# A capped attention with a gated layer behind it: a slightly different hand-written order, a smaller first table, a shorter warm-up, and the last three products in column halves

## The chip, the cores and the metric

The kernel runs on one core of a Trainium2 chip. Its time is device microseconds of one execution; a kernel's time is the median of several runs. Besides, one execution was recorded by the hardware profiler, with a start and a length for every instruction. The engines that matter here are TensorE (products, and weight loads that run beside them), VectorE, ScalarE, GpSimd (little used) and SyncE, whose queue issues most transfers.

## The reference

Four batches of twelve heads, 448 positions, head size 64. The attention's scores are capped by a tanh, and its output goes, heads side by side, through a gated layer whose gate mixes positions:

```python
scores = (1 / sqrt(64)) * q @ k.T
scores = cap * tanh(scores / cap)                # cap = 30
attn = exp(scores - max(scores)); attn /= sum(attn) + 1e-9
x = heads_side_by_side(attn @ v)                 # 4 x 448 x 768

h = gelu_tanh(x @ w_in)                          # 768 -> 1024
u, v = h[..., :512], h[..., 512:]
v_n = (v - mean(v)) / sqrt(var(v) + 1e-6) * g_ln
v_s = w_sg @ v_n + b_sg[:, None]                 # over the 448 positions
out = x + (u * v_s) @ w_out                      # 512 -> 768
```

## The kernel before

The kernel takes two heads (a pair, "batch.pair") at a time, six pairs a batch. Keys stand on the partitions of the scores, in three chunks of 128 and a tail of 64 for two pairs together. For each chunk TensorE makes the scores of both heads (`score`), ScalarE makes a tanh (L615) and an exp (L617) of 128x896 each, and TensorE multiplies by the values (`value`, L576; tails L586). The softmax denominators are made on TensorE too, with a table of ones (`sum`, L468), after VectorE has added some of the exps (`add`, L628). No maximum is subtracted, since the cap bounds the scores.

Most products are made from two rounded parts of each operand, three products for one (`TERMS`); VectorE or ScalarE makes the parts (`qk hi`, L523 or L526, and `qk lo`, L530). Others are plain fp32 products, which need four passes: the values, the sums, score tails (L552), and the scores of a few pairs in the list `PLAIN` (L560).

The gated layer of a batch runs among the attention of the batches that follow: `hv` (L759), `hu` (L814), `vsg` (L831) and `out` (L851) on TensorE, with gelu, layer norm and gate on the other engines between them (`cube` L742, `gelu` L747, `g hi` L306 or L308, `g lo` L334). The weights come as float64 words and are decoded on the chip (lines 380 to 420) while the attention runs.

TensorE's products use four shapes of tile: 128x128 for the gated layer, 64x128 for scores, 128x32 for values and sums, 64x64 for tails. The kernel's program gives each operation the letter of its shape as a mode.

Nothing decides the order at run time. All operations are built first, each with what it reads and writes, and then issued in an order that is written out as the tuple `ORDER`: each entry is twice the operation's number, plus 1 for the second of its two possible engines (ScalarE in place of VectorE). Every engine and every queue keeps its operations in that order and waits at the first whose data isn't there. Costs such as `PASS`, `PASS4` and `ISSUE` are those of the search that made the order; the run doesn't use them.

At the start TensorE runs a few products on zeros (`warm`, L365, `WARM` = 3 products of two records each). The first score's keys come as a small table `first` of their own, with the cap in a 129th column. Three small operations on VectorE (`scales`, L341 to L343) make from the cap the factors that tanh and exp need, and one on GpSimd the factor for the split of queries and keys. The other constants (ones, norm factors) come as a table `consts`. The first pair's queries are issued on ScalarE's queue, all other loads on SyncE's.

At the end the last pair of row blocks goes: `out 5.0` to `out 5.3` of the last batch, each three products of 448 columns into one accumulator; then `residual 5a` and `5b` on VectorE add half the columns each, and a store on SyncE's queue and one on ScalarE's write them out.

## Time and profile before

| | |
|---|---|
| median of 3 runs | 371.4 us (371.33 to 371.82) |
| profiled execution, its own time | 371.88 us |
| its span, first to last instruction | 370.1 us |
| TensorE products busy | 364.8 us |
| VectorE busy | 305.5 us |
| ScalarE busy | 224.1 us |

The span is what the trace covers; about 1.8 us of the execution's time lie around it. A product's end in the trace is modelled and reaches beyond its place in the pipeline, so that the busy time of TensorE also holds short waits. Starts are measured.

### The profile page before, as it was taken

The page shows a single profiled execution, that of the slowest core. Times are in us where ns is not written, and L with a number is a line of the kernel's source. Part 1 is how long each engine was busy: PE and PEld are TensorE (multiplying, and loading weights), DVE is VectorE, ACT ScalarE, POOL GpSimd, SP SyncE. Part 2 cuts the span into 40 slices and gives each one's busy share as a digit, 9 for nine tenths or more (in the row PEclk, how much of TensorE's full clock was granted, in tenths as well). Part 3 has the DMA queues.
Part 4 walks back from the last instruction along what each step waited for, and adds up shares of the span by engine and source line. Part 5 has one row for each costly group of instructions (what it writes and reads, how often), then busy time and mean ns, then how long its engine had stood idle before and what let it go on. Part 6 is the DMA issues. An engine that isn't in the chain of part 4 may idle for free.

```text
span 370.1 us, 6066 instructions
## 1 busy us (share of the span) xinstructions
PE 364.8 (99%) x2324; PEld 248.5 (67%) x2324; DVE 305.5 (83%) x548; ACT 224.1 (61%) x297; POOL 37.6 (10%) x39
## 2 busy tenths in 40 slices
PE   9999999999999999999999999999999999999995
PEld 4333343445778485546558986486889999889995
DVE  3999999999999999999997876986459789167663
ACT  5999999999566878998853528851024330041310
POOL 0303211120301310211000100000001000001000
PEclk9999999999999999999999999999999999999999
DMA  7978254545354214652513401001210000002204
GB/s 268 349 259 279 77 192 167 151 158 160 87 151 128 64 45 139 215 180 69 155 49 115 135 0 49 0 27 60 81 51 25 25 27 26 27 0 75 101 0 149
DMA packets 23996, 39.88 MB, mean 108 GB/s; under 512 B 5568, under 2 KB 18592, under 8 KB 23968
## 3 DMA queue, kind: packets, MB, share of 16 engines
q1 hardware_dynamic: 23680, 39.16, 33.3%
q8 instruction: 18, 0.29, 0.3%
q10 hardware_dynamic: 288, 0.34, 0.3%
q14 instruction: 10, 0.08, 0.1%
HBM read 33.47 MB, written 6.02 MB: 107 GB/s over the span
## 4 chain that ended last, share of the span: by engine, by line
PE 81%; DVE 12%; ACT 2%; issue 2%; DMA 2%; DVEq 0%; ACTq 0%
PE ps L814 12%; PE ps L576 11%; PE ps L851 11%; PE sc L544 9%; PE ps L759 8%; PE ps L831 5%; PE sc L851 5%; PE sc L759 4%; PE sc L814 4%; DVE p L628 3%; PE den L468 3%; PE sc L831 2%; PE sc L552 2%; PE ps L586 2%; DMA n<-spread 2%
## 5 line engine op out<-in xcount | busy, mean ns | idle before, releaser
L617 ACT ACTIVATE p<-p,few 128x896 f32<-128x896 f32 x84 | 85.2, 1047 | 0.5
L628 DVE TENSOR_TENSOR p<-p,p 128x896 f32<-128x896 f32 (+1 forms) x58 | 64.1, 1107 | 4.4 <-PE ps L576 3.0
L615 ACT ACTIVATE p<-sc 128x896 f32<-128x896 f32 x63 | 56.3, 919 | 9.6 <-PE sc L544 6.3
L576 PE MATMUL ps<-p,v 128*32 128x448 f32 x576 | 62.0, 544 | 0.0
L544 PEld LDWEIGHTS sc<-hl 64*128 64x128 f32 x378 | 32.4, 184 | 28.2 <-ACT p L615 15.9
L544 PE MATMUL sc<-hl 64*128 64x448 f32 x378 | 48.8, 385 | 0.0
L814 PE MATMUL ps<-rg,winu 128*128 128x448 f32 x206 | 46.5, 363 | 0.0
L851 PE MATMUL ps<-rg,wout 128*128 128x448 f32 x180 | 45.0, 366 | 0.0
L759 PE MATMUL ps<-winv,rg 128*128 128x512 f32 x170 | 42.6, 391 | 0.0
L814 PEld LDWEIGHTS ps<-rg,winu 128*128 128x128 f32 x206 | 38.5, 188 | 3.3 <-issue 0.3
L413 POOL TENSOR_TENSOR stage<-stage 128x512 int32<-128x512 int32 (+1 forms) x20 | 28.2, 1410 | 113.5 <-DVE stage L403 81.7
L576 PEld LDWEIGHTS ps<-p,v 128*32 128x32 f32 x576 | 15.6, 109 | 35.7 <-issue 20.8
L851 PEld LDWEIGHTS ps<-rg,wout 128*128 128x128 f32 x180 | 33.3, 188 | 5.0 <-issue 1.3
L759 PEld LDWEIGHTS ps<-winv,rg 128*128 128x128 f32 x170 | 31.7, 188 | 7.1 <-DVE rg L334 0.7
L740 ACT ACTIVATE t<-ps 128x448 f32<-128x448 f32 (+1 forms) x22 | 12.5, 567 | 28.6 <-PE ps L814 17.6
L745 ACT ACTIVATE t<-t 128x448 f32<-128x448 f32 (+1 forms) x30 | 18.0, 603 | 19.4 <-DVE t L742 19.3
L774 POOL TENSOR_TENSOR sm<-sm,few 128x1 f32<-128x1 f32 x14 | 8.7, 622 | 182.8 <-DVE sm L772 104.1
L831 PE MATMUL ps<-wsg,rg 128*128 128x448 f32 x116 | 26.7, 366 | 0.0
L740 ACT ACTIVATE t<-sc 128x512 f32<-128x512 f32 (+1 forms) x8 | 4.5, 571 | 34.8 <-PE sc L759 31.9
L530 DVE SCALAR_TENSOR_TENSOR hl<-raw,few,hl 128x848 fp32r<-128x848 f32 x21 | 24.4, 1162 | 0.1
L831 PEld LDWEIGHTS ps<-wsg,rg 128*128 128x128 f32 x116 | 21.5, 188 | 3.2 <-issue 1.0
L615 ACT ACTIVATE p<-sc,few 128x896 f32<-128x896 f32 x21 | 20.9, 1009 | 3.8 <-PE sc L560 1.9
(118 smaller groups left out, 511.8 us busy)
## 6 DMA issues: line engine op xcount, KB each, us to landing
raw<-in_qk_dram SPq DMA_DIRECT2D x22, 456.0 KB
stage<-in_w_in_dram SPq DMA_DIRECT2D x12, 512.0 KB
n<-spread SPq DMA_DIRECT2D x24, 224.0 KB
v<-in_vp_dram SPq DMA_DIRECT2D x24, 192.0 KB
out_dram<-x SPq DMA_DIRECT2D x17, 224.0 KB
stage<-in_w_out_dram SPq DMA_DIRECT2D x8, 384.0 KB
out_dram<-x SPq DMA_DIRECT2D x13, 112.0 KB
u<-in_w_sgT_dram SPq DMA_DIRECT2D x4, 224.0 KB
```

The source lines that it names most:

```text
L413: nc.gpsimd.tensor_tensor(out=a.bitcast(I32), in0=a.bitcast(I32), in1=hi, op=ALU.add)
L530: op(name("qk lo", s), "dve", c_tt(n) + 0.06, lambda: nc.vector.scalar_tensor_tensor(out=part(1), in0=used(), scalar=root, in1=f32(part(0) ...
L544: nc.tensor.matmul(out=sc.t[:, h, :S], lhsT=flat(s, w)[rows, 128 * c - 128:128 * c], rhs=flat(s, m)[rows, Q0 - TL:SQ - TL], start=(k == 0) ...
L576: nc.tensor.matmul(out=pav[s].t[32 * j:32 * j + 32, :S], lhsT=v[s].t[:, 128 * (c - 1) + 32 * j:128 * (c - 1) + 32 * j + 32], rhs=p.t[:, j ...
L615: op(name("tanh", s, c), "act", c_act(2 * S, True, raw_scores), lambda p=p, sc=sc, r=raw_scores: nc.scalar.activation(out=p.t, in_=sc.t[:, ...
L617: op(name("exp", s, c), "act", c_act(2 * S, False, True), lambda p=p: nc.scalar.activation(out=p.t, in_=p.t, func=ACTF.Exp, scale=cap_sb), ...
L628: op(name("add", s, t), "dve", c_tt(2 * S), lambda: nc.vector.tensor_tensor(out=a.t[rows], in0=a.t[rows], in1=p.t[rows], op=ALU.add), rd=[ ...
L745: op(tag + " tanh", "act", c_act(n), lambda: nc.scalar.activation(out=view(), in_=view(), func=ACTF.Tanh, scale=GELU_C * GELU_A), wr=[sq])
L759: nc.tensor.matmul(out=ps.t[:, :HF], lhsT=(xl if a else xh)[c].t[:, t * 128:t * 128 + 128], rhs=win[w][1][:, c, :], start=(c == 0 and k == ...
L814: nc.tensor.matmul(out=ps.t[:, :S], lhsT=win[w][0][:, c, f * 128:(f + 1) * 128], rhs=(xl if a else xh)[c].t[:, :S], start=(c == 0 and k == 0),
L831: nc.tensor.matmul(out=ps.t[:, :S], lhsT=(vl if a else vh)[c].t[:, f * 128:(f + 1) * 128], rhs=wsg[w][:, c, :], start=(c == 0 and k == 0), ...
L851: nc.tensor.matmul(out=ps.t[:, :S], lhsT=wout[w][:, f, c * 128:(c + 1) * 128], rhs=(gl if a else gh)[f].t[:, :S], start=(f == 0 and k == 0 ...
```

## The change

1. `ORDER` is another one. No operation is added but one (below), and what each computes is the same. On TensorE 208 of 525 steps keep their rank and the others move by 1.8 places in the mean, 21 at most. Twenty-five operations change between VectorE and ScalarE, among them the splits `3.1 qk hi`, `3.3 qk hi` and `3.4 qk hi`, which go to ScalarE. On SyncE's queue the constants are issued second, ahead of the keys and queries that had stood before them.
2. The cap moves from the first table, which now has 128 columns (512 bytes a row), into a new last column of the constants. So `scales` reads, and waits for, the constants.
3. The warm-up's products have 272 columns in place of 296.
4. The step `out 5.3` of the last batch becomes `out 5.3a` and `out 5.3b`, three products each on one half of the columns, and `residual 5a` waits for the first half alone.
5. The search's costs `PASS` and `PASS4` are lower.

Some neighbourhoods of the new order that the prediction speaks of, by the names of the steps:

- At the head TensorE's order is score 1, 2, 3, tail score, value 1, then `sum 0` and two scores of pair 0.1; before, value 2 stood ahead of `sum 0`.
- `0 hu 0.0` stood behind `0 hv 2.5`; now three `hu` steps run ahead of that one. On VectorE `1 den sum` and `1 recip` stood ahead of `0 v 0 gelu`; now they come after it.
- On VectorE `2.2 add 0` stood between `0 g lo 1` and `0 g lo 2`; now it comes after `0 g lo 3`. TensorE's `0 out 0.3` reads `g hi 3` and `g lo 3`.
- On TensorE `2 sum 4` stood ahead of `3.0 score 2` and `2.5 value 2`; now both and `2.5 value 3` stand ahead of it.

```diff
--- before.py
+++ after.py
@@ -25,7 +25,7 @@
 COPIES = 4
 PARTS = 64
 WARM = 3
-WCOLS = 296
+WCOLS = 272
 SUMS = (0, 1, 1, 1, 1, 2, 2, 2, 2, 2, 2, 2)
 PLAIN = (1, 0, 0, 1, 0, 0, 0, 0, 0, 0, 0, 0, 1, 0, 0, 0, 0, 0, 0, 0, 0, 0, 0, 0)
 LANES = (17, 18, 19, 20, 21, 22)
@@ -33,89 +33,88 @@
 TPOS = 1
 TPOS0 = 3
 ISSUE = 0.45
-PASS = 0.0165
-PASS4 = 0.003
+PASS = 0.0142
+PASS4 = 0.001
 ORDER = (
-    16, 0, 338, 340, 342, 344, 6, 346, 4, 10, 8, 18, 422, 352, 2, 34, 350, 360, 354, 50, 366, 362, 374, 368, 356, 382,
-    22, 364, 20, 358, 424, 24, 26, 348, 376, 370, 66, 432, 82, 372, 384, 28, 508, 394, 426, 378, 434, 402, 396, 380,
...
+    16, 4, 338, 0, 2, 340, 342, 344, 18, 6, 352, 346, 10, 8, 422, 34, 350, 360, 354, 50, 374, 366, 362, 368, 356, 382,
+    22, 364, 358, 20, 424, 24, 430, 26, 376, 372, 348, 432, 426, 384, 394, 66, 28, 378, 508, 402, 434, 370, 396, 38,
...
+    3086, 3120, 3122, 3134, 3124, 3136, 3126, 3092, 3138, 3104, 3142, 3106, 3128, 3146, 3108, 3094, 3110, 3148, 3096,
+    3112, 3158, 3098, 3150, 3100, 3140, 3160, 3152, 2766, 3162, 3114, 3164, 3154, 3166, 3168, 3156, 3172, 3170, 3174,
 )
 
 
@@ -265,10 +264,11 @@
     for w in range(2):
         win[w][1] = wp.tile([128, KD, HF], FP32R, name=f"winv{w}")
     LO = NP + 31
-    const_sb = wp.tile([128, 2 * LO + KF], FP32, name="const_sb")
+    const_sb = wp.tile([128, 2 * LO + KF + 1], FP32, name="const_sb")
     bsg_sb = wp.tile([128, S], FP32, name="bsg_sb")
     wsg = [wp.tile([128, NC, S], FP32R, name=f"wsg{w}") for w in range(2)]
-    first_sb = wp.tile([128, 129], FP32, name="first_sb")
+    first_sb = wp.tile([128, 128], FP32, name="first_sb")
+    sms.append(small(8, "sm1"))
     d_p = Pool(tiles(1, [PARTS, 2, 2 * NP * S // PARTS], FP32, "d"))
     stages = [wp.tile([128, 1536], FP32, name=f"stage{i}", tag=f"rg{i}") for i in range(RS // 3)]
 
@@ -285,10 +285,10 @@
     n_p = Pool(tiles(NS, [128, S], FP32, "n"))
     raw_p = Pool(tiles(RAWS, [128, SQ], FP32, "raw"))
     Q0 = SQ - S
-    sm_p = Pool(sms + [small(8, f"sm{i}") for i in range(1, 4)])
+    sm_p = Pool(sms + [small(8, f"sm{i}") for i in range(2, 4)])
     ones_sb = const_sb[:, :2 * LO].rearrange("p (k n) -> p k n", k=2)
     g_sb = const_sb[:, 2 * LO:2 * LO + KF]
-    cap_in = first_sb[:, 128:]
+    cap_in = const_sb[:, 2 * LO + KF:]
     sc_p = Pool([pp.tile([128, 2, 512], FP32, name=f"sc{i}") for i in range(2)])
     ps_p = Pool([pp.tile([128, 512], FP32, name=f"ps{i}") for i in range(3)], {"g": 2, "b": 2})
     dsum = [dp.tile([4, NP, S], FP32, name=f"dsum{b}") for b in range(B)]
@@ -334,7 +334,7 @@
         op(tag, "dve", c_tt(n), lambda: nc.vector.tensor_tensor(out=out(), in0=a(), in1=b(), op=ALU.subtract),
            rd=rd, wr=wr, fast=True)
 
-    load("first", lambda: first_sb, lambda: first, [k_first], 70000)
+    load("first", lambda: first_sb, lambda: first, [k_first], 65536)
     load("consts", lambda: const_sb, lambda: consts, [k_const], 60000)
 
     def prepare():
@@ -344,7 +344,7 @@
 
     k_cap, k_root, k_guard = Buf(), Buf(), Buf()
     op("power", "dve", 0.1, lambda: nc.vector.memset(pw, -0.5), wr=[k_pw])
-    op("scales", "dve", 0.4, prepare, rd=[k_first], wr=[k_cap, k_root])
+    op("scales", "dve", 0.4, prepare, rd=[k_const], wr=[k_cap, k_root])
     op("root", "pool", 0.55, lambda: nc.gpsimd.tensor_tensor(out=root, in0=root, in1=pw, op=ALU.pow),
        rd=[k_pw], wr=[k_root], fast=True)
     op("guard exp", "act", 0.3, lambda: nc.scalar.activation(out=guard, in_=cap_sb, func=ACTF.Exp, scale=-1.0),
@@ -845,22 +845,26 @@
 
         def outp(c):
             ps = Buf(ps_p, cls="g")
-            for f in range(KF):
-                def fn(f=f):
-                    for k, (w, a) in enumerate(TERMS):
-                        nc.tensor.matmul(
-                            out=ps.t[:, :S], lhsT=wout[w][:, f, c * 128:(c + 1) * 128],
-                            rhs=(gl if a else gh)[f].t[:, :S], start=(f == 0 and k == 0),
-                            stop=(f == KF - 1 and k == 2))
-                pe("out %d.%d" % (c, f), mms(3), fn, [gh[f], gl[f], chunk["out", f, c * 128 // (DM // 2)]], [ps])
             x = xr[c]
             last = b == B - 1 and c == KD - 1
-            for n, sl in enumerate((slice(0, S // 2), slice(S // 2, S)) if last else (slice(0, S),)):
+            halves = (slice(0, S // 2), slice(S // 2, S)) if last else (slice(0, S),)
+            for f in range(KF):
+                for n, sl in enumerate(halves if f == KF - 1 else (slice(0, S),)):
+                    def fn(f=f, sl=sl):
+                        for k, (w, a) in enumerate(TERMS):
+                            nc.tensor.matmul(
+                                out=ps.t[:, sl], lhsT=wout[w][:, f, c * 128:(c + 1) * 128],
+                                rhs=(gl if a else gh)[f].t[:, sl], start=(f == 0 and k == 0),
+                                stop=(f == KF - 1 and k == 2), skip_group_check=last)
+                    split = last and f == KF - 1
+                    pe("out %d.%d" % (c, f) + ("ab"[n] if split else ""), mms(3, sl.stop - sl.start), fn,
+                       [gh[f], gl[f], chunk["out", f, c * 128 // (DM // 2)]], [(ps, n) if split else ps])
+            for n, sl in enumerate(halves):
                 cols = sl.stop - sl.start
                 eng, queue = ("act", nc.scalar) if n else ("sp", nc.sync)
                 op(name("residual", c) + "ab"[n], "dve", c_tt(cols), lambda sl=sl: nc.vector.scalar_tensor_tensor(
                     out=x.t[:, sl], in0=ps.t[:, sl], scalar=0.5, in1=x.t[:, sl], op0=ALU.mult, op1=ALU.add),
-                   rd=[ps], wr=[(x, sl.start)])
+                   rd=[(ps, n) if last else ps], wr=[(x, sl.start)])
                 parts = 2 if not last and b * KD + c in LANES else 1
                 for m in range(parts):
                     sm = slice(sl.start + cols * m // parts, sl.start + cols * (m + 1) // parts)
@@ -925,11 +929,11 @@
         ones[TL * s:TL * s + TL, 1, NP - 2 + s::NP] = 1.0
     cap = _np.asarray(inputs["cap"], _np.float32).reshape(1, 1)
     consts = _np.concatenate(
-        [ones.reshape(128, -1), inputs["moe_g_ln"].reshape(-1, 128).T], axis=1)
+        [ones.reshape(128, -1), inputs["moe_g_ln"].reshape(-1, 128).T, _np.broadcast_to(cap, (128, 1))], axis=1)
     k2 = byhead(k)
     host = {
         "qk": _np.concatenate([k2[..., 128 * FC:], k2[..., :128 * FC], _np.zeros_like(k2[..., :16]), byhead(q)], axis=3),
-        "first": _np.concatenate([k2[0, 0, :, :128], _np.broadcast_to(cap, (128, 1))], axis=1),
+        "first": k2[0, 0, :, :128],
         "vp": vp,
         "vt": vt,
         "w_in": inputs["moe_w_in"].view(_np.uint64),
```

## Rows read from the trace of the kernel before

**Rows 1.** The page: busy time of the engines, and ScalarE in 40 slices of 9.25 us.

```profile
PE 364.8 (99%) x2324; PEld 248.5 (67%) x2324; DVE 305.5 (83%) x548; ACT 224.1 (61%) x297; POOL 37.6 (10%) x39
...
ACT  5999999999566878998853528851024330041310
```

**Rows 2.** The view of waits: who waited for whom, us in total, times, longest.

```profile
PEld sc L544 <- ACT p L615: 15.9, 24, 0.7
```

**Rows 3.** The timeline of the head: start us, length us, engine, line, operation.

```profile
0.74 0.40 SPq L326 DMA_DIRECT2D first_sb<-in_first_dram  x1
...
2.39 0.34 PEld L365 LDWEIGHTS ps<-const-float32-0.0 128*128 128x128 f32 x1 [0.16 <-issue]
...
2.88 0.34 PEld L365 LDWEIGHTS ps<-const-float32-0.0 128*128 128x128 f32 x1 [0.16 <-issue]
...
3.60 0.16 DVE L341 SCALAR_TENSOR_TENSOR few<-first_sb 128x1 f32<-128x1 f32 x1 [3.60 <-DMA first_sb<-in_first_dram]
...
4.00 0.51 PEld L560 LDWEIGHTS sc<-raw,first_sb 64*128 64x128 f32 x4 [0.78 <-DMA raw<-in_qk_dram]
...
5.92 2.07 ACT L615 ACTIVATE p<-sc,few 128x896 f32<-128x896 f32 x2 [1.92 <-PE sc L560]
...
6.27 0.66 DVE L523 TENSOR_SCALAR hl<-raw,few 128x848 fp32r<-128x848 f32 x1 [2.12 <-DMA raw<-in_qk_dram]
```

**Rows 4.** The chain that ended last, pieces in order of time: start us, length us.

```profile
11.61 1.40 PE sc L544 x12
...
24.06 1.70 PE sc L560 x8
...
31.68 0.81 PE sc L544 x6
...
32.50 2.39 PE ps L576 x24
...
51.72 1.64 PE ps L576 x16
...
54.77 0.89 PE den L468 x8
...
142.00 1.00 DVE p L628
...
172.19 1.15 PE den L468 x8
```

**Rows 5.** The timeline of the tail.

```profile
365.50 0.77 PE L851 MATMUL ps<-rg,wout 128*128 128x448 f32 x3
...
366.30 0.69 DVE L861 SCALAR_TENSOR_TENSOR x<-ps,x 128x224 f32<-128x224 f32 x2 [1.78 <-PE ps L851]
...
367.02 0.35 ACTq L867 DMA_DIRECT2D out_dram<-x  x1
```

**Rows 6.** The timeline near 144 us, TensorE's weight loads.

```profile
144.55 0.19 PEld L851 LDWEIGHTS ps<-r,wout 128*128 128x128 f32 x1 [0.46 <-DVE r L334]
```

**Rows 7.** The timeline near 98 us, VectorE and TensorE's weight loads.

```profile
96.91 0.98 DVE L671 SCALAR_TENSOR_TENSOR d<-d,few 64x84 f32<-64x84 f32 x1
...
97.92 0.67 DVE L674 RECIPROCAL d<-d 64x84 f32<-64x84 f32 x1
...
99.19 0.19 PEld L814 LDWEIGHTS ps<-r,winu 128*128 128x128 f32 x1 [0.95 <-DVE t L747]
...
99.30 0.19 PEld L814 LDWEIGHTS ps<-rg,winu 128*128 128x128 f32 x1
...
99.50 0.19 PEld L814 LDWEIGHTS ps<-r,winu 128*128 128x128 f32 x1
```

**Rows 8.** The timeline near 172 us, VectorE.

```profile
171.25 1.09 DVE L628 TENSOR_TENSOR p<-p,p 128x896 f32<-128x896 f32 x1
```

**Rows 9.** Groups of instructions by form: busy us, mean ns, idle before.

```profile
L523 DVE TENSOR_SCALAR hl<-raw,few 128x848 fp32r<-128x848 f32 x16 | 12.2, 765 | 2.1 <-DMA raw<-in_qk_dram 2.1
...
L526 ACT ACTIVATE hl<-raw,few 128x848 fp32r<-128x848 f32 x5 | 5.0, 996 | 0.9 <-PE sc L544 0.9
```

153 rows, old and new, of the table ORDER are left out of this document.

## The prediction

> **What bounds the kernel now.** I read the page first: TensorE is busy 364.8 of 370.1 us, VectorE and ScalarE clearly less [rows 1]. So the time is the length of TensorE's own list, plus what stands ahead of it and behind it, plus the waits inside it. The view of waits hides the short ones of products, because a product's end is modelled and covers a gap. The weight loads show them better: scores wait on ScalarE's first activation 24 times [rows 2]. Most of these are just in time and cost little; those that reach the products I found by comparing starts in the timeline with the usual spacing.
>
> The head. TensorE warms up on six records of 296 columns, 0.49 us apart, and starts the first score at 4.00 [rows 3]. The first tanh waits for that score until 5.92, and from there ScalarE feeds TensorE almost alone until the next pair's scores at 11.61 [rows 3, 4]. Score 1 takes 1.9 us, at half speed: later two such steps take 1.70 together [rows 3, 4].
>
> The inside. A stretch of value or sum products (128x32 tiles) takes 0.89 us for one operation, 1.64 for two and 2.39 for three [rows 4]: 0.75 each and 0.14 for leaving the tile shape. That is a price for the order alone.
>
> The tail. The last three products start at 365.50, the first half residual at 366.30, both end at 366.99, the last store is issued at 367.02, and 3.0 us of store and closing follow up to 370.1 [rows 5].
>
> **The head of the change.** The warm-up loses 24 of 296 columns: 0.49 x 24/296 = 0.04 us a record, six records, 0.24 us. What it can give is bounded by the data. The keys' small table releases VectorE at 3.60 [rows 3], 2.86 us after its issue; the queries were issued in the same moment on ScalarE's queue and are 224 KB against 64.5. The warm-up's last record starts at 2.88 + 0.49 = 3.37 and streams until 3.86; the score's load follows 0.14 later, which is just the price of leaving a tile shape. So I take the warm-up to be what ends last, with the queries landed a little earlier, and put the gain at **-0.2** (bounds 0, if the queries land at 4.00, and -0.24).
>
> The cap moves from the small table into the constants, whose issue moves from the eighth place on SP's queue to the second, right behind the small table. With that table's own 2.86 us from issue to release, and one issue of 0.40 ahead, they would land near 4.1; three scalings of 0.16 with their gaps follow, so the scale is ready near 4.7, and tanh needs it at 5.7 at the earliest. One us of cover, cost 0; if the constants took twice as long, they would land near 7.0, tanh would start about 1.8 us late, and all behind it. The next pair's queries and keys are passed by one issue, 0.4 us: their split waits for them until 6.27 [rows 3], but its score comes only at 11.61 [rows 4], behind ScalarE. Cost 0; without that cover 0.4. The first values move behind a weight load; their product comes after two tanh, 2.07 us from 5.92 [rows 3], and an exp. Cost 0. Later loads on SP's queue go in another order too; the view of waits names no product but the first that waits for one, and I put that at 0.
>
> **The order.** No operation appears but one more product step, and 25 change between VectorE and ScalarE. Counting both written orders by tile shape: 128x32 stretches fall from 44 to 40, 64x64 stays at 23 stretches, 128x128 at 13, the split scores rise from 41 to 44. Four stretches less save 4 x 0.14 = 0.56. A split score in a stretch of two takes 0.70, and one alone 0.81 [rows 4], with or without a wait in it; so three more cost between 0 and 0.3. I take **-0.5** (bounds -0.26 and -0.56).
>
> Three waits of the kernel before are addressed. (a) Before 144.55 the step out 0.3 waits for the two halves of its operand on VectorE, its last load 0.46 us [rows 6]; the 1.0 us addition of 142.00 that ran ahead of them [rows 4] now comes after, and other work of half its length ahead. I count 0.5. (b) At 99.19 the first hu step waits 0.95 for the gelu on VectorE, which stood behind the denominators' sum and reciprocal, 0.98 and 0.67 [rows 7]. Both now stand behind it, but TensorE also arrives one step earlier, and the gelu still has to wait for its tanh on ScalarE; I count 0.3. (c) The sum step of 172.19 lasts 1.15 where 0.89 is usual [rows 4], as its second operand comes from an addition that ends at 172.34 [rows 8]. The step moves behind two value steps, 1.6 us; 0.26 is won. Together 1.06. But TensorE arrives earlier everywhere, the additions and reciprocals that made room are themselves owed to later steps, and the 24 waits on tanh [rows 2] show how little slack the list has. I keep less than half, **-0.4** (bounds -1.1, all three won, and +1.0, as much lost in new places).
>
> **The tail.** The last three products of 448 columns become six of 224. Products of 448 columns follow each other every 0.20, so half the columns need about 0.10; what I can't read directly is whether its weights load as fast. A load is listed with 0.19 us, yet where loads were free to follow each other they started 0.11 apart: 99.19, then 99.30, and 0.20 when a full product stood between [rows 7]. So I take 0.11 as the spacing. Third product at 365.50 + 0.22, ended after another 0.27: first residual at 366.02 instead of 366.30. Sixth product at 366.05, ended 366.32, second residual at 366.35, ends 366.74 instead of 366.99: **-0.25**, with all of the closing 3.0 us behind it unchanged. With 0.20 a load the sixth starts at 366.50 and the end is 0.20 later. A third price is in the rows: plain fp32 products of 448 columns take 0.85 us for the two of a score step, side by side [rows 4], four times the split ones. If products this narrow lost their fast rate, six of about 0.40 would end at 368.0 and the second residual 1.4 us late. Bounds -0.25 and +1.4.
>
> The Trainium skill speaks against this part ("TensorE: Matmul & The Clock Gate", section LDWEIGHTS): a load costs its columns over 1.2 GHz, 107 ns for 128, however few columns stream through it, so halves make the loads the limit, 0.64 us of six against 0.60 of three. The 0.11 of the trace agrees with it, the 0.19 of its load rows doesn't; by the rule TensorE loses 0.04, and the sum would stand as it is.
>
> Sum: -0.2 - 0.5 - 0.4 - 0.25 = -1.35 on the profiled execution's 371.88, which is 0.48 above the median of 371.4. On the median that is **370.05**, rounded to 370.1.
>
> **The rivals.** *The waits come back.* TensorE is the bound only by a little; each 0.1 saved in its order is met by a split or an exp that isn't ready. For it: the 24 waits on tanh. Against it: VectorE has 17% of the span to spare [rows 1], and the three waits above lie where it was only late with other work. Then head and tail stay, and the order gives nothing: -0.45, 371.0.
>
> *The narrow products are slow.* The tail costs 1.4 instead of winning 0.25: -1.1 + 1.4 = +0.3, 371.7. For it: no row has a split product below 448 columns. Against it: no row shows a product whose rate hangs on its width.
>
> *ScalarE's queue (slower).* Three splits of queries and keys (3.1, 3.3, 3.4) move from VectorE to ScalarE, 996 ns each against 765 [rows 9], in among the tanh and exp that release scores and values. If each delays its neighbours in full, 3.0 us come on top: -1.35 + 3.0 = +1.65, 373.0. It decides from 2.1 us exposed on. For it: ScalarE is busy 8 tenths in the slices of the first two (3 in that of the third) [rows 1], and scores wait for it often. Against it: five such splits already stand there, and the list has other products to run meanwhile.
>
> **How the numbers follow.** A difference of 0.2%, 0.74 us, is about what can be told from none here: faster is below 370.66, slower above 372.14. The forecast has 0.57; its own range, with the order's bounds, is 369.1 to 370.9, so a little of it is no change. Waits come back 0.15 (no change). Narrow products slow 0.18 (mostly no change, some slower). ScalarE's queue 0.10 (slower, seldom in full). Faster 0.55, same 0.31, slower 0.14. The range runs from 369.0, three waits won in full, to 371.9, the slow narrow products with a little more; above it lies ScalarE's queue.
>
> **What would show it.** Right: the first score near 3.8 and the first tanh near 5.7; 40 stretches of 128x32 products; steps out 0.3 and sum 4 at their usual length; half-width products 0.11 apart, the second residual starting 0.8 to 0.9 us after the first narrow product. Wrong: a first score still at 4.00 (the queries bound it); the scalings after 5.5; narrow products 0.2 or 0.4 apart; waits of 0.3 and more on tanh or a split in the stretch from 165 to 205 us. The forecast fails most easily in the waits inside the list, since their size is a judgment and not a row.

## The result, and the profile after

The changed kernel takes 373.82 us (median of 6 runs, 372.51 to 374.15), the kernel before 371.37 (6 runs, 370.44 to 371.82): ratio 1.0055, 95% interval 1.0039 to 1.0071. It is slower, by 2.0 us by the ratio and 2.45 by the medians, and the time lies above the predicted range. The profiled execution took 374.07 us over a span of 372.3; before, 371.88 over 370.1.

The page and the groups by form after show nothing of it: TensorE is as busy as in [rows 1], VectorE less, and ScalarE more by three splits of queries and keys (13 and 8 of them, where [rows 9] has 16 and 5).

```profile
PE 365.1 (98%) x2327; PEld 249.1 (67%) x2327; DVE 301.1 (81%) x545; ACT 227.8 (61%) x300; POOL 40.2 (11%) x39
```

```profile
L523 DVE TENSOR_SCALAR hl<-raw,few 128x848 fp32r<-128x848 f32 x13 | 8.5, 653 | 3.0 <-DMA raw<-in_qk_dram 3.0
...
L526 ACT ACTIVATE hl<-raw,few 128x848 fp32r<-128x848 f32 x8 | 8.0, 997 | 0.0
```

The chain of work that ended last, each piece followed back to what released it, does show it. Here is what it runs over between 26 and 64 us, first in the kernel before and then in the changed one:

```profile
by line: PE ps L576 33.0%; PE sc L544 25.0%; PE den L468 8.6%; PE ps L586 7.2%; PE sc L552 7.2%; issue 5.7%; DVE p L628 5.6%; PE sc L560 2.5%; DVE stage L408 1.9%; DVE d L674 1.7%; DVE hl L523 1.4%; DVE stage L403 0.9%; DVE d L671 0.6%; DVE
```

```profile
by line: DVE p L628 27.4%; DMA stage<-in_w_in_dram 22.9%; issue 14.2%; DVE hl L530 9.2%; DVE x L306 5.8%; DVE hl L523 5.5%; DVE stage L408 5.4%; PE sc L544 5.0%; PE ps L576 4.6%; DVE stage L403 3.8%; DVE stage L397 3.0%; DVE stage L390 2.7%
```

Before, this stretch is nearly all TensorE's own products. After, it is a transfer of weights (`stage<-in_w_in`) and then VectorE's list, one operation after the other. (A piece that reaches into the stretch counts whole, so the shares sum to more than 100%: the transfer runs from 18.79 to 27.50 us, and 1.5 us of it lie in the stretch.) The bound has changed from TensorE to VectorE for 30 us. The view of waits of the same kind, 24 to 64 us, names the handover (after):

```profile
ACT p L615 <- DVE p L628: 3.4, 4, 1.2
...
DVE stage L397 <- DMA stage<-in_w_in_dram: 2.8, 1, 2.8
PEld den L468 <- DVE p L628: 2.0, 3, 1.2
```

None of these three rows is in the view of before for that stretch. The first says that tanh waits for VectorE's additions: an addition frees the buffer that the next tanh writes into.

To weigh the stretches I compared, for every step of TensorE, the time to the next step's start with what is usual, the median of steps of its kind in the kernel before (kept apart by whether the next step has the same tile shape). What is over sums to TensorE's waits, in us:

| stretch, us | before | after | order alone | load put back | early order before, late after |
|---|---|---|---|---|---|
| to 12 | 1.5 | 2.0 | 1.2 | 2.1 | 1.5 |
| 12 to 26 | -0.2 | -0.1 | -0.3 | -0.2 | -0.2 |
| 26 to 64 | 1.1 | 5.0 | 4.0 | 2.9 | 1.1 |
| 64 to 80 | 0.2 | 0.4 | 0.2 | 0.2 | 0.2 |
| 80 to 365 | 3.7 | 2.2 | 2.1 | 2.1 | 2.4 |
| sum | 6.3 | 9.4 | 7.2 | 7.2 | 5.0 |

(The last three columns are `order_only`, `sp_in41` and `splice82` below. Each column is one profiled execution; that of `order_only` took 372.12 us, 1.2 less than its median.) The usual times themselves sum to 355.2 us before and 354.6 after. So the span's +2.2 is: first score 0.24 earlier, tile changes -0.60, waits +3.09, tail -0.04 (from the start of the last products to the end, 4.56 us before and 4.53 after).

**The waits that the prediction named are gone.** After, the loads of `out 0.3` and of the first `hu` step, and the step `sum 4`, as against [rows 6], [rows 7] and [rows 4]:

```profile
147.11 0.19 PEld L855 LDWEIGHTS ps<-r,wout 128*128 128x128 f32 x1
...
101.83 0.19 PEld L814 LDWEIGHTS ps<-rg,winu 128*128 128x128 f32 x1
...
177.31 0.89 PE den L468 x8
```

**Where the new ones start.** SyncE's queue after, and then in `sp_in41`, where only the load `in 4.1` went back ahead of the queries and keys of pair 0.4:

```profile
11.03 0.45 SPq L326 DMA_DIRECT2D stage<-in_w_in_dram  x1
11.79 5.89 SPq L326 DMA_DIRECT2D raw<-in_qk_dram  x2
17.73 1.96 SPq L326 DMA_DIRECT2D stage<-in_w_in_dram  x3
```

```profile
11.22 1.16 SPq L326 DMA_DIRECT2D stage<-in_w_in_dram  x2
12.48 5.28 SPq L326 DMA_DIRECT2D raw<-in_qk_dram  x2
17.82 0.90 SPq L326 DMA_DIRECT2D stage<-in_w_in_dram  x2
```

The second of the two `raw` loads waits for a free buffer and holds the queue until 17.68 (11.79 + 5.89). The weights behind it, three loads where `sp_in41` has two, go out together from 17.73. Load `in 5.1` lands at 27.50 (24.69 before), and VectorE, whose list has a decode step of it at that point, stands still. VectorE and ScalarE after:

```profile
24.28 0.41 DVE L306 CAST winv<-stage 128x512 fp32r<-128x512 f32 x1
27.53 0.43 DVE L397 TENSOR_SCALAR stage<-stage 128x512 f32<-128x512 f32 x1 [2.83 <-DMA stage<-in_w_in_dram]
...
28.88 1.08 DVE L628 TENSOR_TENSOR p<-p,p 128x896 f32<-128x896 f32 x1
...
30.06 1.01 ACT L615 ACTIVATE p<-sc,few 128x896 f32<-128x896 f32 x1 [1.16 <-DVE p L628]
```

The additions behind the decode step come late, the tanh waits for their buffers, and TensorE for the tanh. (Before, the first of these additions started at 25.94, after a wait of 0.52 us for an exp of ScalarE.) VectorE has no slack to catch up: the view by windows has it busy in all of the 13 us from 33 and of the 11 from 46 on, in both kernels. Rows of before, then of after (us of the window, then busy time of PE, PEld, DVE, ACT, POOL):

```profile
26.00:33.00 7.00, 7.00 (x64) 2.44 (x60) 7.00 (x12) 7.00 (x9) 1.42 (x1) 1.00 0.70 210
33.00:46.00 13.00, 13.00 (x122) 4.94 (x112) 13.00 (x20) 13.00 (x16) 3.56 (x2) 1.00 0.46 155
46.00:57.00 11.00, 11.00 (x102) 4.70 (x102) 11.00 (x19) 11.00 (x15) 1.58 (x1) 1.00 0.63 198
```

```profile
26.00:33.00 7.00, 6.27 (x54) 1.78 (x55) 5.47 (x9) 5.64 (x7) 0.00 (x0) 1.00 0.90 324
33.00:46.00 13.00, 13.00 (x118) 5.30 (x116) 13.00 (x23) 12.46 (x15) 1.43 (x1) 1.00 0.56 176
46.00:57.00 11.00, 10.88 (x98) 4.08 (x92) 11.00 (x14) 10.03 (x13) 5.17 (x3) 1.00 0.45 120
```

(ScalarE is as full in the rows of before, so it has no slack there either.)

### The profile page after: what moved, and what is told of

It reads as the page before. It is cut to its first block, busy times and chain, and to the rows that moved or that the text cites. A ratio compares the mean times of both kernels' runs of the same rounds, so it can differ in the third digit from the quotient of the medians.

```text
span 372.3 us, 6079 instructions
## 1 busy us (share of the span) xinstructions
PE 365.1 (98%) x2327; PEld 249.1 (67%) x2327; DVE 301.1 (81%) x545; ACT 227.8 (61%) x300; POOL 40.2 (11%) x39
## 4 chain that ended last, share of the span: by engine, by line
PE 86%; DVE 7%; DMA 3%; issue 2%; SPq 1%; ACT 0%; DVEq 0%
PE ps L759 12%; PE ps L814 12%; PE ps L576 12%; PE ps L855 11%; PE sc L544 10%; PE ps L831 8%; PE sc L855 5%; PE sc L814 4%; PE sc L759 3%; DVE p L628 3%; PE den L468 2%; PE sc L552 2%; DMA stage<-in_w_in_dram 2%; PE ps L586 2%; PE sc L831 2%
## 5 line engine op out<-in xcount | busy, mean ns | idle before, releaser
L576 PE MATMUL ps<-p,v 128*32 128x448 f32 x576 | 62.9, 545 | 0.8 <-ACT p L617 0.3
L544 PE MATMUL sc<-hl 64*128 64x448 f32 x378 | 50.2, 387 | 0.2
L759 PE MATMUL ps<-winv,rg 128*128 128x512 f32 x188 | 47.4, 391 | 0.0
L413 POOL TENSOR_TENSOR stage<-stage 128x512 int32<-128x512 int32 (+1 forms) x20 | 30.7, 1538 | 127.0 <-DVE stage L403 62.2
L855 PE MATMUL ps<-rg,wout 128*128 128x448 f32 (+1 forms) x173 | 41.2, 362 | 0.0
L759 PEld LDWEIGHTS ps<-winv,rg 128*128 128x128 f32 x188 | 35.1, 188 | 7.6 <-DVE rg L306 0.7
L855 PEld LDWEIGHTS ps<-rg,wout 128*128 128x128 f32 x173 | 31.8, 188 | 3.9 <-DVE x L306 0.7
L831 PE MATMUL ps<-wsg,rg 128*128 128x448 f32 x125 | 28.7, 365 | 0.0
L831 PEld LDWEIGHTS ps<-wsg,rg 128*128 128x128 f32 x125 | 23.2, 188 | 3.3 <-DVE sm L769 0.7
L742 DVE SCALAR_TENSOR_TENSOR t<-t,ps 128x448 f32<-128x448 f32 (+1 forms) x23 | 14.9, 650 | 11.4 <-ACT t L740 11.3
```

Of the source, the lines that this page charges most:

```text
L413: nc.gpsimd.tensor_tensor(out=a.bitcast(I32), in0=a.bitcast(I32), in1=hi, op=ALU.add)
L544: nc.tensor.matmul(out=sc.t[:, h, :S], lhsT=flat(s, w)[rows, 128 * c - 128:128 * c], rhs=flat(s, m)[rows, Q0 - TL:SQ - TL], start=(k == 0) ...
L576: nc.tensor.matmul(out=pav[s].t[32 * j:32 * j + 32, :S], lhsT=v[s].t[:, 128 * (c - 1) + 32 * j:128 * (c - 1) + 32 * j + 32], rhs=p.t[:, j ...
L759: nc.tensor.matmul(out=ps.t[:, :HF], lhsT=(xl if a else xh)[c].t[:, t * 128:t * 128 + 128], rhs=win[w][1][:, c, :], start=(c == 0 and k == ...
L831: nc.tensor.matmul(out=ps.t[:, :S], lhsT=(vl if a else vh)[c].t[:, f * 128:(f + 1) * 128], rhs=wsg[w][:, c, :], start=(c == 0 and k == 0), ...
L855: nc.tensor.matmul(out=ps.t[:, sl], lhsT=wout[w][:, f, c * 128:(c + 1) * 128], rhs=(gl if a else gh)[f].t[:, sl], start=(f == 0 and k == 0 ...
```

## The experiments

Times are medians beside the kernel before on the same chip. Moves in the written order are shown as one engine's list, with the names of the steps.

**Order alone, and three ways to undo its early part.** `order_only` is the kernel before with the new `ORDER` and nothing else. The other three start from the changed kernel.

```diff
 sp_in41, SyncE's queue      dve_late_w, VectorE              sp_old, SyncE's queue
  in 3.1 load                -in 5.1 high                     first 40 loads in the order
 +in 4.1 load                 0.4 qk lo, 0.2 add 2            of the kernel before, but
  0.4 qk                     -in 0.0 low, in 0.0 high         the constants stay second
  0.5 qk                      0.5 qk hi
 -in 4.1 load                -in 5.1 shift
  in 5.1 load                 0.2 add 3
                             +in 5.1 high, in 0.0 low
                             +in 0.0 high, in 5.1 shift
```

> The kernel before with the new order alone (old table, 296 columns of warm-up, whole last products). Theory: the loss is all in the new order, in the loads and VectorE's steps of the first 60 us; so this is slower than before by 2.0 to 2.8 us, with VectorE waiting over 2 us for a weight block near 25 us. Rival (the moved cap and constants spoil the head): the order alone is within 0.7 us of before. The scalings read the small first table here, so the first tanh is not tied to the constants.

> The changed kernel with one load moved: the weight block in 4.1 is issued ahead of the queries and keys of pair 0.4 again, as in the kernel before, and so before SP's queue stops for the buffer of 0.5. Theory: in 5.1 and the blocks behind it land about 1.3 us sooner, VectorE's wait near 25 us falls from 2.8 to about 1.5 us, and the time falls by 1 to 2 us. Rival (TensorE's and ScalarE's own new order makes the early waits): within 0.5 us of the changed kernel.

> The changed kernel with four decoding steps of VectorE (in 5.1 high and shift, in 0.0 low and high) moved behind the split and the two additions that stood behind them; loads as they are. Theory: VectorE no longer stands in front of a block that lands at 27.5, the additions come about 2.8 us sooner, TensorE's waits between 28 and 33 us (1.6 us) go and part of those up to 64 us; the time falls by 1.5 to 3.5 us. Rival (the order of the loads delays values, queries and keys directly): TensorE still waits about as long, within 0.7 us of the changed kernel.

> The changed kernel with the first forty loads in the order of the kernel before, but the constants still second, since the scalings need them. Theory: most blocks land when they did before, though VectorE now asks for in 5.1 and in 0.0 earlier than then (in 5.1 landed at 24.7, in 0.0 at 26.1); its wait near 25 us shrinks to about 1 us, and the time falls by 1.5 to 3 us. Rival (TensorE's and ScalarE's own order): within 0.7 us of the changed kernel.

| kernel | median, us | before, us | ratio, 95% interval |
|---|---|---|---|
| order_only | 373.35 (7 runs) | 371.13 | 1.0044 [1.0024, 1.0063] |
| sp_in41 | 371.70 (12) | 371.13 | 1.0012 [0.9998, 1.0025] |
| dve_late_w | 372.12 (12) | 371.13 | 1.0016 [1.0000, 1.0032] |
| sp_old | 371.90 (12) | 371.13 | 1.0015 [1.0001, 1.0029] |

The order alone is slower by as much as the whole change, within the intervals. In its profiled execution VectorE waited 1.5 us for the same block (24 to 64 us, lines one lower) and not over 2, as the block landed at 25.64 and not at 27.50, though SyncE's queue has the same order in both. In `dve_late_w` and `splice82r`, with that order too, it landed at 27.61 and 27.43; why it lands earlier in `order_only` isn't shown.

```profile
DVE stage L396 <- DMA stage<-in_w_in_dram: 1.5, 1, 1.5
```

One load moved back by two places takes 0.43% of 0.55% off, 1.6 us; letting VectorE do other work ahead of the decode that waits for it, or putting the loads in their old order, takes off 0.39% and 0.40%. All three lie in the ranges that were expected or at their lower end, and TensorE's and ScalarE's lists are the same in all three. So this part of the loss is not in TensorE's or ScalarE's own early order, but in VectorE's strict list meeting a late transfer. None of the three is faster than the kernel before, though: the early order has more losses (below). In `sp_in41` VectorE goes through without a wait, where 1.5 us of one were expected to stay, and its addition is 2.9 us earlier:

```profile
24.27 0.41 DVE L306 CAST winv<-stage 128x512 fp32r<-128x512 f32 x1
24.60 0.42 DVE L397 TENSOR_SCALAR stage<-stage 128x512 f32<-128x512 f32 x1
...
25.96 1.07 DVE L628 TENSOR_TENSOR p<-p,p 128x896 f32<-128x896 f32 x1
```

**The head.** `pad129` and `consts3` start from `sp_in41`.

```diff
 pad129
-    first_sb = wp.tile([128, 128], FP32, name="first_sb")
+    first_sb = wp.tile([128, 129], FP32, name="first_sb")
 consts3, SyncE's queue
  first
- consts
  0.0 qk 1
+ consts
```

> The version with the load of 4.1 put back, and the first table's rows padded from 128 columns (512 bytes) to 129 (516 bytes); the cap stays in the constants, which keep their 79 columns. Theory that the size of the first table's rows decides how late the first keys land: keys of 0.0 land near 4.5 us instead of 5.99, tanh 2 starts near 6.6 instead of 7.0, the run is 0.2 to 0.4 us shorter than the same version without the padding. Rival, the constants' longer rows (316 bytes) or their place right ahead of the keys are the cause: keys still near 5.9, time the same.

> The version with the load of 4.1 put back, and on SyncE's queue the constants issued behind the first pair's keys (0.0 qk 1) instead of ahead of them. Theory that the constants ahead of the keys cost the head its gain: the keys are issued at 1.2 instead of 1.65 and land near 4.4 instead of 5.5 to 6.1, score 2 starts near 5.1 instead of 5.6 to 6.2, the scale is still ready for tanh 1 at 5.3, and the run is 0.5 to 0.9 us shorter than with the load alone. Rival, that the size of the first table's rows (512 bytes, kept here) delays what follows it: the keys still land over 5.3, time the same. If tanh 1 waits for the scale beyond 5.6, the gain is halved.

The rows after show why the earlier start came to nothing, against [rows 3]:

```profile
0.74 0.40 SPq L326 DMA_DIRECT2D first_sb<-in_first_dram  x1
...
1.20 0.41 SPq L326 DMA_DIRECT2D const_sb<-in_consts_dram  x1
1.65 1.38 SPq L326 DMA_DIRECT2D raw<-in_qk_dram  x3
...
3.76 1.16 PE L560 MATMUL sc<-raw,first_sb 64*128 64x448 f32 x4
3.88 0.16 DVE L341 SCALAR_TENSOR_TENSOR few<-const_sb 128x1 f32<-128x1 f32 x1 [3.01 <-DMA const_sb<-in_consts_dram]
...
4.97 1.01 ACT L615 ACTIVATE p<-sc,few 128x896 f32<-128x896 f32 x1 [0.69 <-PE sc L560]
...
5.93 1.77 PE L560 MATMUL sc<-raw 64*128 64x448 f32 x8 [1.02 <-DMA raw<-in_qk_dram]
...
7.00 1.01 ACT L615 ACTIVATE p<-sc,few 128x896 f32<-128x896 f32 x1 [1.03 <-PE sc L560]
```

The first score and tanh are early, but score 2 waits for the first pair's own keys, which land at 5.89 (4.22 before), and tanh 2 starts at 7.00, where it had started at 6.98. In `pad129` those keys landed at 5.15 and the time was 371.67 (ratio 1.0014 [1.0002, 1.0026]); in `consts3` at 4.29, and the time was 371.81 (1.0018 [1.0009, 1.0027]). With 128 columns and the new constants ahead of them the keys landed at 5.25 to 6.16 in nine kernels, so taking the constants away from there brings the keys forward. But in `order_only` the constants are ahead of the keys as well, with the old rows (516 bytes of the table, 312 of the constants in place of 316), and the keys landed at 4.47. So the place alone isn't what delays them; which of the row sizes has a part stays open, and 5.15 with 516 and 316 bytes doesn't decide it. That the late keys cost the run anything isn't shown either, since neither kernel is shorter than `sp_in41`. In `consts3` tanh 2 started at 7.06 for all its early keys: there the clock rose late (last section).

**GpSimd beside VectorE.** What is left in `sp_in41` near there is a wait of 1.0 us inside `1 sum 0`, whose second half reads the additions of pair 1.0, and one of 0.4 inside `1.2 score 1`, which follows it. In the changed kernel the same place reads (GpSimd, VectorE, ScalarE, TensorE):

```profile
52.77 3.10 POOL L413 TENSOR_TENSOR stage<-stage 128x512 int32<-128x512 int32 x2 [2.72 <-DVE stage L408]
...
54.62 2.19 DVE L628 TENSOR_TENSOR p<-p,p 128x896 f32<-128x896 f32 x1
...
57.41 1.07 DVE L628 TENSOR_TENSOR p<-p,p 128x896 f32<-128x896 f32 x1
...
58.57 0.92 ACT L615 ACTIVATE p<-sc 128x896 f32<-128x896 f32 x1 [0.74 <-DVE p L628]
...
58.53 0.95 PE L468 MATMUL den<-p,const_sb 128*32 128x448 f32 x4 [0.40 <-DVE p L628]
```

The addition `1.0 add 2` takes 2.19 us beside GpSimd's integer addition; its like takes 1.07. I moved the step that releases GpSimd, `in 2.0 sign`, in VectorE's list, and then gave 40 steps of that list their old order:

```diff
 sign_late           sign_later          dve_mid
- in 2.0 sign       - in 2.0 sign        40 steps, in 2.0 low to 1.2 add 3,
  1.0 add 2           1.0 add 2          in the relative order that they
  1.0 add 3           1.0 add 3          have in the kernel before
+ in 2.0 sign         1.2 qk lo
  1.2 qk lo         + in 2.0 sign
```

> The version with the load of 4.1 put back, and one step of VectorE, the sign of decode 2.0, moved from ahead of 1.0 add 2 to behind 1.0 add 3; GpSimd's addition, which waits for it, then starts after both adds. Theory that VectorE's add is stretched because GpSimd's addition runs beside it: 1.0 add 2 takes 1.1 us instead of 2.2, add 3 ends about 1.7 us earlier, the two waits of tanh of 0.73 us on these adds go, and TensorE's 1.3 us wait near 57 us falls below 0.4; the run is 0.5 to 1.3 us shorter. Rival, that the add is slow for a reason of its own (its operands): it stays at 2.2 us and the waits at 0.7; time the same.

> The version with the load of 4.1 put back, and VectorE's sign step of decode 2.0 moved further still, behind 1.2 qk lo, so that GpSimd's additions run beside neither the adds of 1.0 nor that split. Theory that whatever stands beside GpSimd's addition is stretched, and that the last try only handed the stretch from the add to the split: 1.0 add 2 and 1.2 qk lo both take 1.1 us, TensorE's wait of 1.0 us before 1.2 score 0 goes, its waits between 57 and 64 us sum to under 0.8 us (2.4 in the version it starts from, 1.5 in the last try), 0.6 to 1.5 us shorter unless a later step takes it back. Rival, that the wait has another cause, such as VectorE being full here: it stays over 0.8 us.

> The version with the load of 4.1 put back, and the 40 steps of VectorE from the decode in 2.0 low to 1.2 add 3 in the kernel before's relative order; all other engines as they are. Theory that VectorE's decode steps ahead of the adds of 1.0 cost what is left: TensorE's waits between 57 and 64 us fall from 1.75 to under 0.8 us, and the run is 0.7 to 1.3 us shorter than with the load alone, ratio 0.998 to 0.9995. Rival, that VectorE is full from 46 to 80 us in either order, so that the wait only moves: waits of 1.5 us or more between 57 and 80 us, ratio 1.001 or more.

`sign_late` took 372.63 us, ratio 1.0042 [1.0030, 1.0055]; `sign_later` 372.60, 1.0040 [1.0027, 1.0053]; `dve_mid` 372.75, 1.0048 [1.0036, 1.0061]. All are slower than what they start from. The stretch did move with GpSimd; in `sign_late`:

```profile
54.52 3.47 POOL L413 TENSOR_TENSOR stage<-stage 128x512 int32<-128x512 int32 x2 [6.04 <-DVE stage L408]
...
50.99 1.09 DVE L628 TENSOR_TENSOR p<-p,p 128x896 f32<-128x896 f32 x1 [0.88 <-ACT p L617]
...
54.68 2.15 DVE L530 SCALAR_TENSOR_TENSOR hl<-raw,few,hl 128x848 fp32r<-128x848 f32 x1
56.76 1.52 DVE L397 TENSOR_SCALAR stage<-stage 128x512 f32<-128x512 f32 x1
```

The addition is back at 1.09, and now the split takes 2.15 and a conversion 1.52 (0.41 usual). `1.2 score 1` waits for that split, again 1.0 us, and 0.7 us more are lost at 74 us. In `sign_later` the stretch has moved on to the next split, 1.70 us, and a cast, 1.52. The wait of 1.0 us is gone, as expected, but TensorE stands for as long a little later, up to 64.14, for an addition of VectorE, and 0.7 us are lost at 74 us here too:

```profile
64.14 0.96 PE L468 MATMUL den<-p,const_sb 128*32 128x448 f32 x8 [1.23 <-DVE p L628]
```

In `dve_mid` the waits that end between 57 and 64 us fall to 0.23 us, and 2.1 come between 48 and 57 and 1.3 between 64 and 80: its rival, that VectorE is full and the wait only moves, came true. So the stretch by GpSimd is shown, and the repair fails: VectorE has no free time there, and a move within its list only decides who waits.

**Three splits back on VectorE, from `sp_in41`.**

```diff
- 3.1 qk hi, 3.3 qk hi, 3.4 qk hi on ScalarE
+ 3.1 qk hi, 3.3 qk hi, 3.4 qk hi on VectorE
```

> The version with the load of 4.1 put back, and the three splits 3.1, 3.3 and 3.4 qk hi back on VectorE, as in the kernel before. The rival named in the prediction (ScalarE's queue, up to 3.0 us): 0.5 to 3.0 us shorter. Theory that these three cost nothing where they are, as no product waits between 165 and 205 us: time the same within 0.3 us, or a little longer.

372.56 us, ratio 1.0040 [1.0027, 1.0052]: slower than `sp_in41`. The rival falls, and the theory that they cost nothing either way as well: in this order they win on ScalarE. Its trace shows 0.34 us more of waits between 150 and 200 us, less than the times differ, so where the rest is lost isn't shown.

**Warm-up and tail alone, on the kernel before; then the residual built first.**

```diff
 warm_tail
-WCOLS = 296
+WCOLS = 272
- out 5.3
+ out 5.3a, out 5.3b
 res_early, from warm_tail: the order of building
  out 5.3a
+ residual 5a
  out 5.3b
- residual 5a
```

> The kernel before with its own order, its own first table and constants, and only the shorter warm-up (272 columns) and the last products in halves. By the prediction's steps: 0.2 + 0.25 = 0.45 us shorter, first score at 3.8. By the reading of the changed kernel's trace: the head's gain is lost again before the second tanh, and the second residual starts only 0.05 to 0.1 us earlier, so 0.1 to 0.3 us shorter, which five rounds can hardly tell from none. If the first score waits for its queries, it starts at 4.0 still.

> The kernel before with the shorter warm-up and the halved last products, and the first half's residual built ahead of the products of the second half instead of behind them; each engine's own list is the same. Theory that the residual in the changed kernel waits for a mark that only the last of the six products sets: now it has its own mark, starts about 0.6 us after the first narrow product instead of 0.86, and the second residual starts 0.25 us earlier than there, so that the run is 0.2 to 0.3 us shorter. Rival, the residual is late for another reason (the accumulator's end): same starts, same time.

`warm_tail` took 370.92 us beside 371.05: ratio 1.0000 [0.9991, 1.0010]. `res_early` took 371.72 beside 371.29: 1.0015 [1.0007, 1.0024], slower where 0.2 to 0.3 us were expected to be won. In the changed kernel the six products start at 367.752, .854, .966, 368.075, .188 and .299, and both residuals come behind the last of them (first row). In `res_early` the first residual is early, and the second half's products wait for it (the other rows):

```profile
368.61 0.69 DVE L865 SCALAR_TENSOR_TENSOR x<-ps,x 128x224 f32<-128x224 f32 x2 [1.24 <-PE ps L855]
```

```profile
364.61 0.49 PE L855 MATMUL ps<-rg,wout 128*128 128x224 f32 x3
365.14 0.39 DVE L865 SCALAR_TENSOR_TENSOR x<-ps,x 128x224 f32<-128x224 f32 x1 [1.50 <-PE ps L855]
...
365.58 0.59 PE L855 MATMUL ps<-rg,wout 128*128 128x224 f32 x3 [0.48 <-DVE x L865]
```

Both halves write one accumulator, and the rows show that the program orders a write of it behind an earlier read of it. With the residual built last it waits for all six; built first, it stops the other three. Either way the halves don't overlap: from the first narrow product to the end of the second residual it takes 1.55 us in the changed kernel, where the three whole products and their residuals took 1.49 [rows 5].

**All of the undone parts together** (`sp_in41`, `consts3`, `sign_later` and `res_early` in one kernel):

> All of the undone parts together on the changed kernel: the load of 4.1 put back, the constants behind the first keys, the sign step of decode 2.0 behind 1.2 qk lo, the residual ahead of the second half's products. If the losses found so far are the whole of what took back the new order's gain, the run is 1.0 to 2.5 us shorter than the kernel before (ratio 0.993 to 0.997). If waits come back elsewhere, as the rival of the prediction has it, within 0.4 us of the kernel before.

372.71 us, ratio 1.0038 [1.0024, 1.0052]: it missed, as two of its four parts lose by themselves.

**The two halves of the order.** TensorE's first 101 steps behind the warm-up, to `1 sum 6`, are the same set in both orders. (That step starts at 86.25 us in the trace of before and at 90.29 after; the names and the expectations have 82.)

```diff
 splice82, on warm_tail
  the order of before to 1 sum 6
- the order of before behind it
+ the order of after behind it
 splice82r, on the changed kernel
  the order of after to 1 sum 6
- the order of after behind it
+ the order of before behind it
```

> The kernel before with the shorter warm-up and the halved last products, in its own order on all engines up to TensorE's step 1 sum 6 (82 us), and the changed kernel's order behind that. Theory that the changed order loses only ahead of 64 us and wins behind it: it keeps the early order's waits (2.6 us up to 80 us) and takes the late one's (2.1 to 2.2 us instead of 3.7 from there on) with 0.25 us less of tile changes, so about 1.7 us shorter than the kernel before, 369.5, ratio 0.995. Rival, that the early loss and the late gain hang together (TensorE arriving later finds its operands ready, so the late waits are few only because the early ones were many): the late waits return to about 3.5 us, ratio 0.999 to 1.000.

> The reverse: the changed kernel with its own order up to TensorE's step 1 sum 6 and the order of the kernel before behind it. Theory of an early loss and a separate late gain: it has the early loss in full and not the gain, 375 us, ratio 1.010. Rival, that both hang together: the late waits stay few, 373.8, ratio 1.0055 as the changed kernel.

`splice82` took 369.85 us (369.43 to 369.99, 5 runs) beside 371.20: ratio 0.9963 [0.9951, 0.9975], faster than both kernels. `splice82r` took 374.79: 1.0085 [1.0058, 1.0111], slower than both. Early loss and late gain are two things and nearly add up: against `warm_tail`'s 1.0000 the late half of the new order is worth -0.37% and the early half (with the moved cap) +0.85%, together +0.48%, and the whole change measured +0.55%. The chain of `splice82` (its lines are one lower) between 26 and 64 us is TensorE's again:

```profile
by line: PE ps L575 39.2%; PE sc L543 32.4%; PE den L467 10.9%; PE ps L585 9.6%; PE sc L551 7.2%; PE sc L559 2.5%
```

## Why the prediction was wrong, step by step

**The step that failed** is "Later loads on SP's queue go in another order too; the view of waits names no product but the first that waits for one, and I put that at 0." It asked only whether TensorE waits for a load. VectorE does: a decode step stood in its list for 2.83 us, and ScalarE's tanh and TensorE behind it. By `sp_in41` it cost about 0.43% of 371, 1.6 us, where the prediction had 0.

**The early order beyond that load** is the second step that failed. The case against the rival of returning waits was that VectorE has 17% of the span to spare. That is a mean: between 26 and 57 us VectorE had nothing to spare before either. So the early half, without the gains elsewhere, cost 0.85%, some 3.1 us; 1.5 to 1.8 of it are left when the load is put back. The traces put the waits of that rest behind VectorE's additions and splits near pair 1.0, some of them stretched by GpSimd, but no move there won it back, so what causes it is argued and not shown.

**The waits won (-0.4).** All three are gone as described, and I was too timid: in the traces 0.53 us between the starts of `out 0.2` and `out 1.1`, 0.81 over the three steps around the first `hu`, 0.26 at `sum 4`. With the tile changes behind `1 sum 6`, 0.25, the late half won 1.35 us by the times of `splice82`. The bound of 1.1 was nearer than the value taken. Losses in new places, bounded at +1.0, came too, but as three times that, and in the early half, which I had not looked at for waits of VectorE.

**The order's shape (-0.5)** measured -0.60.

**The head (-0.2).** The first score started at 3.76, as foretold; the scalings ran from 3.88, with their cover, and the first tanh at 4.97, where 5.7 was foretold, as the clock had risen. The step overlooked that the constants pass the first pair's own keys and not only the next pair's, and in the changed kernel's trace the gain was gone at the second tanh. But warm-up and halves together measured nothing in `warm_tail` either, where the keys landed at 4.21; so the 0.24 us came to nothing without that delay too, and where they go stays open.

**The tail (-0.25)** measured -0.04. The spacing of 0.11 was right, and narrow products keep their rate, so that rival falls. What failed was "first residual at 366.02 instead of 366.30": the first residual waits for all six products. The halves themselves won nothing (1.55 us for 1.49); what little was won is in the closing behind them.

**ScalarE's queue** was wrong in its sign, by `splits_dve`. The rival of returning waits was the right one to name, but it was priced at a lost gain of 0.9, and its bound of +1.0 was too small; so the range ended at 371.9. (The "own range" of 369.1 to 370.9 doesn't follow from the bounds: on 371.4 these sum to 369.25 and, with narrow products at their rate, to 371.89.) No sign of being wrong that was listed came, as all of them lay at the head, at the tail or between 165 and 205 us, and the loss lay between 26 and 64.

## What to carry to other kernels

Where engines keep a written order, a transfer counts as late for every engine whose list has a step on it, so look at waits for DMA on the engines that decode and split as well as on the one that bounds the span. Read the slack of an engine in the stretch that changes, by windows, and not from its share of the span. And when an order as a whole loses, cut it where both orders have done the same steps: here one half was worth keeping.

## What the hardware showed

Operations of VectorE on SBUF, with one input or two, are stretched when they start beside one of GpSimd's additions: 2.19 us where 1.07 is usual, 2.15 for 1.09, 1.52 for 0.41. Not every operation is: a copy out of the accumulators (PSUM) keeps its 0.6 us beside an addition of GpSimd (`sp_in41`, first two rows), and in `sign_late` it is GpSimd's addition that takes 3.10 us in place of 1.3 to 1.7 (last row), while the split that VectorE starts at 46.19, beside it, keeps its 1.12.

```profile
50.61 3.12 POOL L413 TENSOR_TENSOR stage<-stage 128x512 int32<-128x512 int32 x2 [2.71 <-DVE stage L408]
...
51.03 0.61 DVE L306 COPY x<-ps 128x448 f32<-128x448 f32 x1
```

```profile
45.38 3.10 POOL L413 TENSOR_TENSOR stage<-stage 128x512 int32<-128x512 int32 x1 [9.46 <-DVE stage L408]
```

The Trainium skill ("SBUF — State Buffer", section "SBUF: two separate sides") says that the two engines share a pair of ports as an exclusive lock, which VectorE needs for an operation with two inputs from SBUF or in one of its two-port modes, and that whichever comes second is blocked for the whole of the other's instruction. The rows agree: in the changed kernel GpSimd's two additions end at 55.87 us, and VectorE's addition that had been issued at 54.62 ends 0.94 us after that.

TensorE's granted clock rose from 1.2 to 2.4 GHz at 4.07 us in the profile after and at 6.36 in that of before, and between 4.37 and 6.77 in the other kernels, behind the same six warm-up products, 24 columns more or less. Score 1, the same four products, took 1.21 us to its tanh after and 1.92 before. Tanh 2 started at 6.21 in `warm_tail`, where the clock rose at 4.76, and at 6.98 before. So the heads of single profiles can't be compared to within 0.7 us; the times of many runs can.
